# Expert lists scattered into DRAM slots, and gate logits and ranks in a PSUM bank of their own

## The chip, the cores and the metric

The kernel runs on one core of a Trainium2 chip. The metric is device time in microseconds (us). The kernel before took 1025.91 us, the median of 3 executions (1025.23 to 1027.11). Engines are named as the profile names them: PE (matrix multiply), PEld (its weight load), DVE (vector), ACT (scalar), POOL, SP (which issues most DMAs).

## The reference

Local attention in chunks of 64 tokens over 8 heads of 64, for 8 x 576 = 4608 tokens, gives x of 512 values per token. A mixture of 8 experts follows, of which each token uses two:

```
logits = x @ w_gate
noise_scale = np.log1p(np.exp(x @ w_noise))
noisy_logits = logits + noise_scale * noise
top2 = np.argpartition(-noisy_logits, 2, axis=1)[:, :2]
top2_w = softmax over the two                      # (shortened)
for e in range(E):
    for k in range(2):
        mask = top2[:, k] == e
        h = np.maximum(x[mask] @ w1[e], 0.0)       # 512 -> 1024
        out[mask] += top2_w[mask, k, None] * (h @ w2[e])   # 1024 -> 512
```

All of it is in 32-bit floats. To know which rows an expert gets, the kernel needs for each expert a list: which token stands in its slot 0, 1, 2 and so on, with which weight.

## The kernel before

**Attention.** Tokens go in 36 tiles of 128. `attend(it)` is a software pipeline: in one call it issues scores (L407), max, subtract and exp (L411, L416, L419) of tile `it`, the transpose of an older tile, the product with v (L434) and the normalisation on DVE (L439, L442, L446) of older ones still, then the transpose (L454) and the store of x to the DRAM buffer `xbuf`. Every fourth call issues the gate matmul (L461, L472). PSUM has 8 banks: scores in 0 and 1, the product with v in 3 and 4, the gate matmul in 6. The gate's logits and the ranks stand in the free columns of bank 3 or 4, by turns with the group. PE, DVE and ACT guard PSUM against each other by whole banks.

**Routing.** Tokens are routed in five groups of 8, 8, 4, 8, 8 tiles. `route(g)` is a generator: each `next` issues a small piece, so that it lies between attention's instructions (`step_route`, 10 steps in an attend). It finds the two experts (MAX, MAX_INDEX), counts by two kinds of matmuls how many earlier tokens chose each expert (rank), and writes `lii` (L572), the slot number of each token and choice: rank times 8 plus the expert. `vals` holds the pair to be listed, token number and weight.

**Lists.** A list is built by one-hot matmuls. Per token tile POOL (L595) and ACT (L596, L597) make one-hot matrices of the slot's row, DVE (L599) one-hots of its column and expert, POOL (L603; DVE for the last group) multiplies these with `vals`, and PE adds 128x160 products in PSUM bank 7 (`place`, L587). The profile has 4 rows of L587 for a tile, 144 in all. At a group's end DVE adds the bank into `acc` (L619, L621). `EARLY` starts expert 0 before all groups are known: block 0 after group 1, block 1 after group 3, block 2 after group 4. `finish_lists` (L202 to L206, DVE) turns list entries into row numbers and weights; `gather` (L235, POOL) fetches the rows by indirect DMA. After the last group four DVE pairs (L634, L636) sort the lists by expert size, and `finish_lists` runs for all lists; `pieces` then computes the row numbers for later gathers (L255).

**Experts.** Each expert has 1152 to 1216 slots in blocks of about 384. `layer1` makes 8 slices (f) of h, each 4 x 3 matmuls (three products of high and low parts in reduced precision, L300), then ACT writes hh (L318) and DVE hl (L319), its low part. `layer2` makes a tile of 128 rows from 8 slices; DVE weighs it (L338), POOL stores it by an indirect DMA that adds (L267). Layer 1 of block 0 issues the last attends from a hook, with a step of routing in the other hooks; layer 2 of block 0 and layer 1 of block 1 step the routing too. `finish_route` issues what is left before layer 2 of block 1.

**Order.** The schedule is manual: each engine runs its instructions in the order in which the code issues them and waits for semaphores. An instruction that waits holds up all behind it on its engine. SP's DMAs stand in one queue: loads of q, k and v, weights of expert 0, zeroing of the output (L665, 37 of 256 KB), then the later weights.

Of the kernel before, what the change touches and what calls it, by code (L numbers as in the profile page):

```python
# [8 lines left out]
FT = mybir.dt.float32  # L9
# [10 lines left out]
P = 128  # L20
# [3 lines left out]
NE = 8  # L24
# [36 lines left out]
def kernel(ctx, tc, qT, kT, vh, wgn, noise, w1, w2, out, caps=CAPS):  # L61
# [18 lines left out]
    row = consts.tile([P, P], FT, name="row")  # L80
    nc.gpsimd.iota(row, pattern=[[1, P]], base=0, channel_multiplier=0, allow_small_or_imprecise_dtypes=True)
    e_row = row[:, 0:NE]

    row_p = consts.tile([P, P], FT, name="row_p")
    nc.gpsimd.iota(row_p, pattern=[[NE, P]], base=0, channel_multiplier=0, allow_small_or_imprecise_dtypes=True)
    row_je = consts.tile([P, NLIST, NE], FT, name="row_je")
    nc.gpsimd.iota(row_je, pattern=[[NE * P, NLIST], [1, NE]], base=0, channel_multiplier=0, allow_small_or_imprecise_dtypes=True)
# [76 lines left out]
    NL = NJ * NE  # L164
    acc = consts.tile([P, 2, NL], FT, name="acc")
# [12 lines left out]
    opieces = out.rearrange("r (q c) -> (r q) c", c=P)  # L178
    HF = {}
# [210 lines left out]
    nc.sync.dma_start(xbuf[0:P, :], zero)  # L390
    load_q(3)
# [26 lines left out]
    def soft_exp(t):  # L418
        nc.scalar.activation(PR[t], PR[t], AF.Exp, scale=0.125)  # L419
# [45 lines left out]
    def lg_at(t):  # L465
        g = grp_of[t]
        c = 264 + 16 * (t - groups[g][0])
        return PS[:, 3 + g % 2, c:c + 16]
# [7 lines left out]
    def route(g):  # L476
# [8 lines left out]
        lg = PS[:, 3 + g % 2, 264:264 + 16 * G].rearrange("p (g a e) -> p g a e", a=2, e=NE)  # L485
# [45 lines left out]
        rk = PS[:, 3 + g % 2, 400:400 + 8 * (G + 1)].rearrange("p (g e) -> p g e", e=NE)  # L531
# [43 lines left out]
        pj = gate.tile([P, 2, 2, G], I32, name="gpj")  # L575
        pf = gate.tile([P, 2, 2, G], FT, name="gpf")
        V.tensor_scalar(pj[:, 0], lii[:, :, ts], NE * (P - 1), None, op0=OP.bitwise_and)
        V.tensor_tensor(pj[:, 1], lii[:, :, ts], pj[:, 0], OP.subtract)
        V.tensor_copy(pf, pj)  # L579
        yield  # L580

        lp = PS[:, 7, 0:2 * NL]
        built = []

        def place(r, ohp, rhs):
            for k in range(2):
                nc.tensor.matmul(lp, ohp[:, k], rhs[:, k].rearrange("p c n -> p (c n)"),  # L587
                                 start=(r == 0 and k == 0), stop=(r == G - 1 and k == 1))

        B = nc.gpsimd if g < LAST else V  # L590
        n2 = [P, 2, NL]
        for r in range(G):
            t = t0 + r
            ohp = gate.tile([P, 2, P], FT, name="gohp", bufs=3)
            nc.gpsimd.tensor_scalar(ohp[:, 0], row_p, pf[:, 0, 0, r:r + 1], None, op0=OP.is_equal)  # L595
            nc.scalar.activation(ohp[:, 1], row_p, AF.Abs, scale=-1.0, bias=pf[:, 0, 1, r:r + 1])  # L596
            nc.scalar.activation(ohp[:, 1], ohp[:, 1], AF.Relu, scale=-1.0, bias=1.0)  # L597
            eq = gate.tile(n2, FT, name="geq", bufs=3)
            V.tensor_tensor(eq, row_je.rearrange("p j e -> p (j e)")[:, None, :].to_broadcast(n2),  # L599
                            pf[:, 1, :, r:r + 1].to_broadcast(n2), OP.is_equal)  # L600
            yield
            rhs = gate.tile([P, 2, 2, NL], FT, name="grhs", bufs=3)
            B.tensor_tensor(rhs, eq[:, :, None, :].to_broadcast([P, 2, 2, NL]),  # L603
                            vals[:, :, t, :, None].to_broadcast([P, 2, 2, NL]), OP.mult)
            yield
            yield
            built.append((r, ohp, rhs))
            if len(built) > 2:
                yield
                place(*built.pop(0))  # L610
            yield
        while built:
            for _ in range(3):
                yield
            place(*built.pop(0))
        yield
        av = acc.rearrange("p c n -> p (c n)")
        if g == 0:
            V.tensor_copy(av, lp)  # L619
        else:  # L620
            V.tensor_add(av, av, lp)  # L621
        a4 = acc.rearrange("p c (j e) -> p c j e", e=NE)
        for i in EARLY:
            if g == EARLY[i]:
                js = slice(blocks[0][i][0][0], blocks[0][i][-1][0] + 1)
                finish_lists(lid0[i], lwt0[i], lfl[:, js, 0], a4[:, :, js, 0])
                gather(i)
        if g == LAST:
            for c in range(2):
                for js in (slice(0, NJ // 2), slice(NJ // 2, NJ)):  # L630
                    n = [P, js.stop - js.start, NE, NE]
                    by = gate.tile([P, 2, 2, NL], FT, name="grhs", bufs=3).rearrange("p a b n -> p (a b n)")
                    by = by[:, 0:n[1] * NE * NE].rearrange("p (j r e) -> p j r e", r=NE, e=NE)
                    V.tensor_tensor(by, a4[:, c, js][:, :, None, :].to_broadcast(n),  # L634
                                    perm[:, None].to_broadcast(n), OP.mult)
                    V.tensor_reduce(accp[:, c, js], by, AX.X, OP.add)  # L636
                    yield
            finish_lists(lid, lwt, lfl, accp)
# [14 lines left out]
    def finish_route(until=lambda: not routing):  # L653
        while not until():
            step_route(1)

# [10 lines left out]
    def attend(it):  # L667
# [58 lines left out]
    def hook_tail(f, d):  # L726
        if d == 0 and f % 2 == 0 and f >= 2:
            if f == 2:
                zero_out(10)
            zero_out(9)  # L730
        if d % 2 and tail and (f, d) != (0, 3):
            attend(tail.pop(0))
        else:
            step_route(2)

    for i in range(NBL + 1):
# [40 lines left out]
        if i < NBL:  # L777
            layer1(i, hook1, hook_tail if i == 0 else lambda f, d: step_route(1))
# [160 lines left out]
```

## Time and profile before

| | |
|---|---|
| Median of 3 (lowest to highest) | 1025.91 us (1025.23 to 1027.11) |
| Profiled execution | 1026.64 us |
| its span | 1024.7 us |
| its mean granted PE clock | 0.977 |
| PE busy | 970.7 us (95%) |
| DVE, ACT, POOL busy | 461.7, 300.8, 475.5 us |

The profile is one execution. Its page gives busy times and groups of instructions by line; L12 is line 12 of the kernel before. "Idle before" is the time in which the engine stood before instructions of this group, with what ended it. A timeline row is start, duration, engine, line, operation, tiles, and in brackets the idle time just before and its releaser.

### The profile page before, as it was taken

Reading aid. Unit: us, or ns where it says so; the run is one execution under the profiler, and the core shown is the slowest. Engines: PE = TensorE matmul, PEld = TensorE weight load, DVE = VectorE, ACT = ScalarE, POOL = GpSimd, SP = SyncE. Lnnn points to the kernel's source line nnn. Section 1 sums busy time; section 2 is a strip of 40 time slices with the busy share of each in tenths; the row PEclk is TensorE's granted clock in tenths of the full one; section 3 lists DMA queues with packets and bytes.
Section 4 is the critical chain, followed back from the end, with each engine's and each line's share of the span. In section 5 each row is a group of like instructions: output and inputs, shape, how many; then the busy total and the mean of one; then the engine's idle time right before and its main releaser. Section 6 shows DMA issues by size and latency. Waiting matters only on the chain.

```text
span 1024.7 us, 18328 instructions
## 1 busy us (share of the span) xinstructions
PE 970.7 (95%) x7353; PEld 864.3 (84%) x7353; DVE 461.7 (45%) x1037; ACT 300.8 (29%) x649; POOL 475.5 (46%) x613
## 2 busy tenths in 40 slices
PE   6888978999799999999999999999999999999995
PEld 4677757898679899889988998899989998899884
DVE  5587765644334444344424533453245334434311
ACT  3466644331223232123212321231123222323100
POOL 1043523425767467436743775378336734611111
PEclk9889989999899999999999999999999999999998
DMA  9997891232251335233533353335333434412213
GB/s 365 397 326 275 302 380 43 46 95 75 60 141 44 88 89 137 49 82 90 135 49 83 98 128 55 83 101 126 55 104 97 98 66 105 124 27 31 32 21 42
DMA packets 51943, 121.51 MB, mean 119 GB/s; under 512 B 8288, under 2 KB 9184, under 8 KB 51856
## 3 DMA queue, kind: packets, MB, share of 16 engines
q0 software_dynamic: 20160, 38.69, 20.6%
q1 hardware_dynamic: 26512, 72.20, 19.3%
q10 hardware_dynamic: 5184, 9.44, 2.4%
q8 instruction: 58, 0.95, 0.4%
q14 instruction: 29, 0.24, 0.1%
HBM read 81.56 MB, written 38.73 MB: 117 GB/s over the span
## 4 chain that ended last, share of the span: by engine, by line
PE 87%; DVE 5%; DMA 3%; issue 2%; ACT 1%; SPq 1%; POOL 0%; DVEq 0%; ACTq 0%
PE PS L300 79%; DMA out<-zero 2%; PE PS L587 1%; PE PS L434 1%; PE PS L407 1%; SPq L665 1%; PE PS L423 1%; PE PS L329 1%; DVE xs L446 1%; DVE pr L416 1%; DVE mx L411 1%; PE PS L454 1%; PE PS L472 1%; DMA st<-in_w 1%; PE PS L461 0%
## 5 line engine op out<-in xcount | busy, mean ns | idle before, releaser
L255 POOL DMA_INDIRECT xg<-xbuf,piece x257 | 259.4, 1009 | 77.2 <-issue 62.3
L300 PE MATMUL PS<-xh,w1h 128*128 128x384 f32 (+2 forms) x768 | 264.0, 344 | 4.3 <-issue 1.9
L300 PE MATMUL PS<-xh,w1l 128*128 128x384 f32 (+2 forms) x768 | 261.9, 341 | 2.5 <-issue 2.5
L300 PE MATMUL PS<-xl,w1h 128*128 128x384 f32 (+2 forms) x768 | 262.1, 341 | 1.6 <-issue 1.3
L300 PE MATMUL PS<-w2h,hh 128*128 128x512 f32 x584 | 228.7, 392 | 0.0
L300 PE MATMUL PS<-w2h,hl 128*128 128x512 f32 x584 | 227.8, 390 | 0.1
L300 PE MATMUL PS<-w2l,hh 128*128 128x512 f32 x584 | 227.7, 390 | 0.0
L267 POOL DMA_INDIRECT out<-o,lid x73 | 116.8, 1600 | 227.8 <-DVE o L338 208.8
L319 DVE SCALAR_TENSOR_TENSOR hl<-PS,hh 128x384 fp32r<-128x384 f32 (+1 forms) x192 | 107.1, 559 | 246.1 <-ACT hh L318 185.2
L318 ACT ACTIVATE hh<-PS 128x384 fp32r<-128x384 f32 (+1 forms) x192 | 94.0, 491 | 374.7 <-PE PS L300 316.7
L300 PEld LDWEIGHTS PS<-xh,w1h 128*128 128x128 f32 x768 | 145.2, 189 | 9.0 <-issue 3.8
L300 PEld LDWEIGHTS PS<-xl,w1h 128*128 128x128 f32 x768 | 145.1, 189 | 5.4 <-issue 3.0
L300 PEld LDWEIGHTS PS<-xh,w1l 128*128 128x128 f32 x768 | 145.2, 189 | 3.4 <-issue 2.4
L338 DVE TENSOR_SCALAR o<-PS,lwt 128x512 f32<-128x512 f32 x73 | 54.5, 749 | 190.3 <-PE PS L300 153.5
L300 PEld LDWEIGHTS PS<-w2h,hl 128*128 128x128 f32 x584 | 109.2, 187 | 23.9 <-issue 0.5
L300 PEld LDWEIGHTS PS<-w2h,hh 128*128 128x128 f32 x584 | 109.2, 187 | 23.1 <-issue 0.8
L300 PEld LDWEIGHTS PS<-w2l,hh 128*128 128x128 f32 x584 | 109.2, 187 | 22.8 <-issue 0.4
L290 ACT ACTIVATE xh<-y 128x512 fp32r<-128x512 f32 x67 | 41.2, 614 | 101.2 <-DVE y L287 72.8
L291 DVE TENSOR_TENSOR xl<-y,xh 128x512 fp32r<-128x512 f32 x67 | 44.9, 671 | 48.0 <-ACT xh L290 33.5
L595 POOL TENSOR_SCALAR gohp<-row_p,gpf 128x128 f32<-128x128 f32 x36 | 24.2, 674 | 71.8 <-DVE gpf L579 54.2
L287 DVE STREAM_TRANSPOSE y<-xg 128x512 f32<-128x512 f32 x67 | 45.6, 680 | 0.0
L136 DVE TENSOR_TENSOR w2l<-st,w2h 128x512 fp32r<-128x512 f32 x64 | 44.5, 695 | 0.0
(138 smaller groups left out, 788.6 us busy)
## 6 DMA issues: line engine op xcount, KB each, us to landing
st<-in_w SPq DMA_DIRECT2D x64, 512.0 KB
out<-zero SPq DMA_DIRECT2D x37, 256.0 KB
vb<-in_vh SPq DMA_DIRECT2D x18, 520.0 KB
qp<-in_qT SPq DMA_DIRECT2D x18, 512.0 KB
kb<-in_kT SPq DMA_DIRECT2D x18, 512.0 KB
xbuf<-xs ACTq DMA_DIRECT2D x36, 256.0 KB
xg<-xbuf,piece POOLq DMA_INDIRECT x257
out<-o,lid POOLq DMA_INDIRECT x73
```

The costliest lines, as they stand in the source:

```text
L136: (eng or nc.vector).tensor_sub(lo[:, s], st[:, s], hi[:, s].bitcast(FT))
L255: nc.gpsimd.indirect_dma_start(out=XG[e, j][:, t * P:(t + 1) * P], out_offset=None, in_=xpieces, in_offset=bass.IndirectOffsetOnAxis(ap=pi ...
L267: s = nc.gpsimd.indirect_dma_start(out=to, out_offset=bass.IndirectOffsetOnAxis(ap=rows, axis=0), in_=o, in_offset=None, compute_op=OP.add)
L287: nc.vector.transpose(y[:, 0:4 * r], x[:, 0:4 * r])
L290: nc.scalar.activation(oh, src, AF.Copy)
L291: nc.vector.tensor_sub(ol, src, oh.bitcast(FT))
L300: nc.tensor.matmul(p, a, b, start=first and n == 0, stop=last and n == 2)
L318: nc.scalar.activation(hh[:, 0:m], p, AF.Relu)
L319: nc.vector.scalar_tensor_tensor(hl[:, 0:m], p, 0.0, hh[:, 0:m].bitcast(FT), op0=OP.max, op1=OP.subtract)
L329: nc.tensor.matmul(p[32 * q:32 * q + 32, 0:P], HF[0][:, f, 32 * t:32 * t + 32], w[:, q * P:(q + 1) * P], start=(f == 0), stop=(f == NF - 1))
L338: nc.vector.tensor_scalar(o[0:r], p[0:r], weights_of(i, j)[0:r], None, op0=OP.mult)
L595: nc.gpsimd.tensor_scalar(ohp[:, 0], row_p, pf[:, 0, 0, r:r + 1], None, op0=OP.is_equal)
```

## The change

The list matmuls and everything that feeds them (L574 to L621) are removed. After `lii` is written, 16 (group 2: 8) entries go into a FIFO of closures, `moves`. Each is `place_one(t, k)`: a POOL memset of one element and an indirect DMA that writes 128 rows of 8 bytes, (token, weight), from `vals` to the DRAM tensor `lists` at the slots `lii[:, k, t]`: 72 scatters. They are declared independent of each other. A DMA of SP at the start zeroes the slots (82 KB). After the scatters of groups 1 and 3 follow an SP DMA that reads expert 0's part into `acc0[i]`, five empty moves, and finish_lists with gather; after those of group 4 an SP DMA of all lists into `acc` (128 x 10 runs of 64 bytes), five empty moves, finish_lists and gather for block 2, the four reorder pairs as moves, and the full finish_lists. Moves are taken 3 at a time in an attend, one in each hook of layer 1 of block 0, and one in every second hook of layer 2 of block 0 and layer 1 of block 1. Logits and ranks are moved into bank 7, which has no other use until `pieces`.

```
-        lg... PS[:, 3 + g % 2, 264 + ...]          rk = PS[:, 3 + g % 2, 400:...]
+        c = 128 * (g % 2) + 16 * (t - groups[g][0])
+        return PS[:, 7, c:c + 16]
+        rk = PS[:, 7, 256:256 + 8 * (G + 1)]...
...
+    nc.sync.dma_start(slots.rearrange("(p a) c -> p (a c)", p=P), zero[:, 0:2 * NJ * NE])
...
-        for r in range(G):
-            ... gohp (L595 to L597), geq (L599), grhs (L603), place (L587)
-        V.tensor_copy(av, lp) / V.tensor_add(av, av, lp)
+        moves.extend(lambda t=t, k=k: place_one(t, k) for t in range(t0, t0 + G) for k in range(2))
         for i in EARLY:
-            if g == EARLY[i]:
-                finish_lists(...); gather(i)
+            if g == EARLY[i] and g < LAST:
+                moves.append(lambda i=i, js=js: read.append(nc.sync.dma_start(acc0[i], by_slot[:, js, 0, :])))
+                moves.extend([None] * 5)
+                moves.append(lambda i=i, js=js: (finish_lists(lid0[i], lwt0[i], lfl[:, js, 0], acc0[i]...), gather(i)))
         if g == LAST:
+            moves.append(lambda: nc.sync.dma_start(acc.rearrange("p j e c -> p j (e c)"),
+                                                   by_slot.rearrange("p j e c -> p j (e c)")))
+            moves.extend([None] * 5)
+            ... finish_lists and gather(2), four reorder moves, finish_lists(lid, lwt, lfl, accp)

+    def place_one(t, k):
+        nc.gpsimd.memset(spacer, 0.0)
+        d = nc.gpsimd.indirect_dma_start(
+            out=lists, out_offset=bass.IndirectOffsetOnAxis(ap=lii[:, k, t:t + 1], axis=0),
+            in_=vals[:, k, t, :].bitcast(I32), in_offset=None)
...
+        step_moves(3 if it <= NT else 0)         # attend, after soft_exp
+        step_moves(1)                            # hook_tail (layer 1 of block 0)
+            step_moves(1 - f % 2)                # hook2_r (layer 2 of blocks 0 and 1)
+  lambda f, d: (step_route(1), step_moves(1 - d % 2))   # layer 1 of block 1
```

The order of instructions moves at three places (lines of the changed kernel are shifted by one to three: L200 to L204 there are finish_lists, L410, L415 and L438 to L445 the attention's DVE work, L317 is hl, L336 the weighing). First DVE in attention, where the list of block 0 is finished. Before, behind the normalisation in the attend of tile 31 and ahead of that tile's max; `acc` is the sum of the list matmuls:

```order
L446 TENSOR_TENSOR xs<-PS,rc 128x2x4x64
L621 TENSOR_TENSOR acc<-acc,PS 128x160
L202 COPY lwt_121<-acc 128x3
L203 TENSOR_SCALAR lfl<-acc,col 128x3
L204 SCALAR_TENSOR_TENSOR lfl<-acc,lfl 128x3
L205 TENSOR_SCALAR lfl<-lfl,col 128x3
L206 CAST lid_118<-lfl 128x3
L411 TENSOR_REDUCE mx<-PS 128x8
L416 TENSOR_TENSOR pr<-PS,mx 128x2x4x64
```

The changed kernel, after tile 33's subtraction; `acc_111` is `acc0[0]`, which SP's read fills, and the copy waits for that DMA:

```order
L410 TENSOR_REDUCE mx<-PS 128x8
L415 TENSOR_TENSOR pr<-PS,mx 128x2x4x64
L200 COPY lwt_119<-acc_111 128x3
L201 TENSOR_SCALAR lfl<-acc_111,col 128x3
L202 SCALAR_TENSOR_TENSOR lfl<-acc_111,lfl 128x3
L203 TENSOR_SCALAR lfl<-lfl,col 128x3
L204 CAST lid_116<-lfl 128x3
L438 TENSOR_SCALAR rc<-PS 128x8
```

The list of block 0 moves nearly three attends later in the order, and what follows on DVE is the normalisation (L438) in the attend of tile 34. Group 1's `lii` moves one attend earlier.

Second, DVE in layer 1 of block 1, where the list of block 2 is finished. Before, behind hl of the last slice:

```order
L319 SCALAR_TENSOR_TENSOR hl_3142<-PS,hh_3141 128x384
L621 TENSOR_TENSOR acc<-acc,PS 128x160
L202 COPY lwt_123<-acc 128x4
L203 TENSOR_SCALAR lfl<-acc,col 128x4
L204 SCALAR_TENSOR_TENSOR lfl<-acc,lfl 128x4
L205 TENSOR_SCALAR lfl<-lfl,col 128x4
L206 CAST lid_120<-lfl 128x4
```

The changed kernel, from hl of slice 4 (`hl_2992`) to hl of slice 6 (`hl_2996`):

```order
L317 SCALAR_TENSOR_TENSOR hl_2992<-PS,hh_2991 128x384
L200 COPY lwt_121<-acc 128x4
L201 TENSOR_SCALAR lfl<-acc,col 128x4
L202 SCALAR_TENSOR_TENSOR lfl<-acc,lfl 128x4
L203 TENSOR_SCALAR lfl<-lfl,col 128x4
L204 CAST lid_118<-lfl 128x4
L317 SCALAR_TENSOR_TENSOR hl_2994<-PS,hh_2993 128x384
L589 TENSOR_TENSOR gby<-acc,gperm 128x320
L591 TENSOR_REDUCE gaccp<-gby 128x40
```

The copy from `acc` now stands ahead of hl of slices 5 to 7, with the reorder pairs between these. The list of block 1 likewise stands between hl of slices 4 and 5 of layer 1 of block 0 (before between slices 6 and 7).

Third, POOL where the gather of block 2 stands (`lid_118` is its list in the changed kernel). It follows the last scatters, five of which stand behind the third store of block 0:

```order
L607 MEMSET spacer 1x1
L608 DMA lists<-vals,lii 44032x2
L233 DMA xg<-xbuf,lid_118 128x512 x3
L233 DMA xg<-xbuf,lid_118 64x512
L264 MEMSET spacer 1x1
L265 DMA out<-o,lid_117 4736x512
```

Before, the last one-hots of POOL stood there:

```order
L595 TENSOR_SCALAR gohp<-row_p,gpf 128x128 x5
L235 DMA xg<-xbuf,lid_120 128x512 x3
L235 DMA xg<-xbuf,lid_120 64x512
L266 MEMSET spacer 1x1
L267 DMA out<-o,lid_119 4736x512
```

So on POOL scatters take the places of one-hots, ahead of the same gathers and stores. On SP the read for block 0 stands between the first and second w2 load of expert 0, that for block 1 behind 28 of the 37 zeroing DMAs, and that of all lists behind the w1 loads of expert 1.

More of the change, by code (lines that the diff above doesn't have):

```diff
@@ L79 @@
     spacer = consts.tile([1, 1], FT, name="spacer")
-    row = consts.tile([P, P], FT, name="row")
-    nc.gpsimd.iota(row, pattern=[[1, P]], base=0, channel_multiplier=0, allow_small_or_imprecise_dtypes=True)
+    row = consts.tile([P, NE], FT, name="row")
+    nc.gpsimd.iota(row, pattern=[[1, NE]], base=0, channel_multiplier=0, allow_small_or_imprecise_dtypes=True)
     e_row = row[:, 0:NE]
[L84 to L87, printed above, removed]
     vals = consts.tile([P, 2, NT, 2], FT, name="vals")
@@ L161 @@
     xg = ctx.enter_context(tc.tile_pool(name="xg", bufs=5))
-    NL = NJ * NE
-    acc = consts.tile([P, 2, NL], FT, name="acc")
+    acc = consts.tile([P, NJ, NE, 2], FT, name="acc")
+    acc0 = {b: consts.tile([P, len(blocks[0][b]), 2], FT, name=f"acc0{b}") for b in EARLY if EARLY[b] < 4}
     lid = consts.tile([P, NJ, NE], I32, name="lid")
@@ L178 @@
     opieces = out.rearrange("r (q c) -> (r q) c", c=P)
+    slots = lists[0:NJ * P * NE, :].bitcast(FT)
+    by_slot = slots.rearrange("(j p e) c -> p j e c", p=P, e=NE)
+    placed, read = [], []
     HF = {}
@@ L466, in lg_at @@
         g = grp_of[t]
-        c = 264 + 16 * (t - groups[g][0])
-        return PS[:, 3 + g % 2, c:c + 16]
+        c = 128 * (g % 2) + 16 * (t - groups[g][0])
+        return PS[:, 7, c:c + 16]
     def gate_sum(g):
@@ L530, in route @@
             yield
-        rk = PS[:, 3 + g % 2, 400:400 + 8 * (G + 1)].rearrange("p (g e) -> p g e", e=NE)
+        rk = PS[:, 7, 256:256 + 8 * (G + 1)].rearrange("p (g e) -> p g e", e=NE)
         nc.tensor.matmul(rk, before, ohb, start=True, stop=False)
@@ L574, in route @@
         yield
[L575 to L579, printed above, removed]
-        yield
[L582 to L588, printed above, removed]
@@ L590, in route @@
-        B = nc.gpsimd if g < LAST else V
-        n2 = [P, 2, NL]
-        for r in range(G):
[L593 to L623, printed above, removed]
-            if g == EARLY[i]:
-                js = slice(blocks[0][i][0][0], blocks[0][i][-1][0] + 1)
-                finish_lists(lid0[i], lwt0[i], lfl[:, js, 0], a4[:, :, js, 0])
-                gather(i)
@@ L628, in route @@
[L628 to L638, printed above, removed]
+        moves.extend(lambda t=t, k=k: place_one(t, k) for t in range(t0, t0 + G) for k in range(2))
@@ new lines, in route, with reorder @@
+        for i in EARLY:
+            if g == EARLY[i] and g < LAST:
+                js = slice(blocks[0][i][0][0], blocks[0][i][-1][0] + 1)
+                moves.append(lambda i=i, js=js: read.append(nc.sync.dma_start(acc0[i], by_slot[:, js, 0, :])))
+                moves.extend([None] * 5)
+                moves.append(lambda i=i, js=js: (finish_lists(lid0[i], lwt0[i], lfl[:, js, 0], acc0[i].rearrange("p j c -> p c j")),
+                                                 gather(i)))
+        if g == LAST:
+            a4 = acc.rearrange("p j e c -> p c j e")
+            def reorder(c, js):
+                n = [P, js.stop - js.start, NE, NE]
+                by = gate.tile([P, NJ * NE * NE // 2], FT, name="gby", bufs=2)
+                by = by[:, 0:n[1] * NE * NE].rearrange("p (j r e) -> p j r e", r=NE, e=NE)
+                V.tensor_tensor(by, a4[:, c, js][:, :, None, :].to_broadcast(n),
+                                perm[:, None].to_broadcast(n), OP.mult)
+                V.tensor_reduce(accp[:, c, js], by, AX.X, OP.add)
+            moves.append(lambda: nc.sync.dma_start(acc.rearrange("p j e c -> p j (e c)"),
+                                                   by_slot.rearrange("p j e c -> p j (e c)")))
+            moves.extend([None] * 5)
+            for i in EARLY:
+                if EARLY[i] == LAST:
+                    js = slice(blocks[0][i][0][0], blocks[0][i][-1][0] + 1)
+                    moves.append(lambda i=i, js=js: (finish_lists(lid0[i], lwt0[i], lfl[:, js, 0], a4[:, :, js, 0]), gather(i)))
+            moves.extend(lambda c=c, js=js: reorder(c, js) for c in range(2) for js in (slice(0, NJ // 2), slice(NJ // 2, NJ)))
+            moves.append(lambda: finish_lists(lid, lwt, lfl, accp))
@@ new lines, in route @@
+        yield
+    moves = []
+    def place_one(t, k):
[3 more added lines that the diff above has]
+            in_=vals[:, k, t, :].bitcast(I32), in_offset=None)
+        for o in placed:
+            tc.declare_no_dep(d.ins, o.ins, reason="each token and expert has a slot of its own")
+        for o in read:
+            tc.declare_no_dep(d.ins, o.ins, reason="slots that were read are not written afterwards")
+        placed.append(d)
@@ L640, with step_moves @@
+    def step_moves(n):
+        for _ in range(n):
+            if moves:
+                move = moves.pop(0)
+                if move:
+                    move()
     routing = []
@@ L651, with finish_route @@
     ordered = []
-    def finish_route(until=lambda: not routing):
+    def finish_route(until=lambda: not routing and not moves):
         while not until():
             step_route(1)
+            step_moves(1)
     halves = [(c, h) for c in range(4) for h in range(2)]
@@ L734, in hook_tail @@
             step_route(2)
+        step_moves(1)
     for i in range(NBL + 1):
@@ L777 @@
         if i < NBL:
-            layer1(i, hook1, hook_tail if i == 0 else lambda f, d: step_route(1))
+            layer1(i, hook1, hook_tail if i == 0 else lambda f, d: (step_route(1), step_moves(1 - d % 2)))
         split1 = halves if (i < NBL and b == nb - 1 and e + 1 < NE) else []
```

2 lines of the change are left out of this document (1 added, 1 removed).

## The prediction

> **What bounds the kernel now.** I read the busy line first, then a table of stretches, the groups, the chain of waits in the attention stage, and the timelines of PE, POOL and DVE. The table's columns are the stretch in us, its length, and each engine's busy time and instructions, then the granted clock, the DMA share and GB/s.
>
> ```profile
> PE 970.7 (95%) x7353; PEld 864.3 (84%) x7353; DVE 461.7 (45%) x1037; ACT 300.8 (29%) x649; POOL 475.5 (46%) x613
> ...
> 38.00:70.00 32.00, 27.23 (x658) 22.68 (x657) 23.77 (x82) 18.93 (x39) 7.64 (x6) 0.87 0.99 371
> 75.00:100.00 25.00, 22.43 (x526) 18.29 (x516) 19.29 (x71) 16.10 (x39) 9.38 (x13) 1.00 0.81 275
> 100.00:125.00 25.00, 23.59 (x493) 20.15 (x491) 17.53 (x53) 15.91 (x40) 10.71 (x16) 0.93 0.84 291
> 125.00:150.00 25.00, 19.44 (x367) 14.80 (x365) 17.30 (x67) 12.57 (x31) 8.45 (x11) 0.86 1.04 392
> 187.00:208.00 21.00, 19.76 (x102) 15.87 (x101) 14.52 (x73) 4.82 (x12) 8.50 (x11) 1.00 0.32 63
> 208.00:247.00 39.00, 37.85 (x216) 34.77 (x214) 17.94 (x45) 9.19 (x21) 13.47 (x15) 1.00 0.35 95
> 247.00:275.00 28.00, 22.20 (x88) 17.65 (x87) 6.74 (x11) 4.14 (x8) 19.70 (x26) 0.82 0.28 58
> 275.00:1024.70 749.70, 737.45 (x3969) 667.98 (x3967) 298.41 (x494) 182.00 (x380) 380.04 (x484) 0.99 0.35 82
> ```
>
> From 275 us on PE is busy 98% of the time, with work that the change doesn't touch. So the answer is decided before: attention until 149 us, then expert 0's first blocks to 250. There PE is at 78 to 94% in attention and 94 to 97% between 187 and 247. List work is on PE's chain in the stage where the lists are built, 73.1 to 112 us:
>
> ```profile
> by line: PE PS L587 13.2%; PE PS L423 10.3%; PE PS L434 9.8%; PE PS L407 9.7%; PE PS L454 7.2%; DVE xs L446 5.3%; DVE mx L411 4.7%; issue 4.5%; PE PS L472 4.2%; DVE pr L416 3.2%; DVE gmi L515 2.9%; ACT xt L455 2.8%; PE PS L461 2.6%; ACT pts
> ```
>
> **What is removed.** The groups give the list work that goes (busy us, mean ns):
>
> ```profile
> L587 PE MATMUL PS<-grhs,gohp 128*128 128x160 f32 x144 | 25.1, 306 | 0.8 <-POOL grhs L603 0.8
> L595 POOL TENSOR_SCALAR gohp<-row_p,gpf 128x128 f32<-128x128 f32 x36 | 24.2, 674 | 71.8 <-DVE gpf L579 54.2 <-PE PS L587 16.4 <-ACT xt L455 1.2
> L603 POOL TENSOR_TENSOR grhs<-geq,vals 128x320 f32<-128x320 f32 x28 | 20.4, 728 | 2.6 <-DVE geq L599 2.2 <-DVE rc L439 0.3
> L596 ACT ACTIVATE gohp<-row_p,gpf 128x128 f32<-128x128 f32 x36 | 14.2, 396 | 22.2 <-DVE gpf L579 12.1 <-PE PS L587 10.0
> L599 DVE TENSOR_TENSOR geq<-row_je,gpf 128x160 f32<-128x160 f32 x36 | 12.1, 345 | 0.2
> L439 DVE TENSOR_SCALAR rc<-PS 128x8 f32<-128x8 f32 x36 | 5.7, 159 | 16.7 <-PE PS L472 13.9 <-PE PS L434 2.7
> ```
>
> The 306 ns is not the price on PE, since starts overlap. PE's timeline (start, us) shows it, together with the pace of attention, whose tiles start with L407 (tiles 10, 18, 19 and 35), and the first work of expert 0's blocks (L283).
>
> ```profile
> 39.55 1.13 PE L407 MATMUL PS<-kb,qp 64*64 64x64 f32 x32
> 68.26 0.69 PE L407 MATMUL PS<-kb,qp 64*64 64x64 f32 x32
> 73.14 0.86 PE L407 MATMUL PS<-kb,qp 64*64 64x64 f32 x32
> 76.95 1.35 PE L587 MATMUL PS<-grhs,gohp 128*128 128x160 f32 x8
> 142.12 0.69 PE L407 MATMUL PS<-kb,qp 64*64 64x64 f32 x32 [1.06 <-DVE pr L416]
> 149.09 1.09 PE L283 MATMUL PS<-ident,xg 128*128 128x128 f32 x8
> ...
> 172.06 0.70 PE L587 MATMUL PS<-grhs,gohp 128*128 128x160 f32 x4
> 172.49 0.45 PE L300 MATMUL PS<-xh,w1h 128*128 128x384 f32 x1
> 172.78 0.34 PE L300 MATMUL PS<-xl,w1h 128*128 128x384 f32 x1
> 172.95 0.34 PE L300 MATMUL PS<-xh,w1l 128*128 128x384 f32 x1
> ```
>
> Attention: groups 0 to 2 hold 20 token tiles, 4 rows each, 80 rows by 1.35/8 = 0.17 us: 13.5 us of PE. By pace: tiles 10 to 18 take (68.26 - 39.55)/8 = 3.59 us each without list matmuls, tiles 19 to 35 take (142.12 - 73.14)/16 = 4.31; 0.72 by 16 = 11.5. I take **12**. In the layers a tile's 4 rows push the next matmul back by 0.43 (172.06 to 172.49) and stretch it by 0.29 - 0.17 = 0.12; 16 tiles (groups 3 and 4) by 0.55 = **9**. The list work of POOL, ACT and DVE lies beside this in the pace, and is not counted again.
>
> Logits and ranks in bank 7: rc waited 13.9 us for L472, a gate matmul that shares its bank. Between 0 (PE was 90% busy around it) and 13.9; PE itself seldom waited there, so I take **1**. The new bank is shared by logits and ranks of adjacent groups, both off the attention chain: 0.
>
> Other edits at nothing: the zeroing of 82 KB at the start lies under loads; the smaller iotas run ahead of the first tile. The DMA engines look full (1.04), but 37 zeroing transfers of 256 KB, 9.7 MB, are in it and are due only before the first store. Without them, 75 to 150 us moved 25 x (275 + 291 + 392) = 23.9 less 9.7 MB, 14.2 MB; in 62 us that is 229 GB/s against the 371 seen. The cover gone, that is rival two.
>
> **What is added.** 72 scatters of 128 rows of 8 bytes, each with a memset, in POOL's order. Before has no plain scatter; the nearest rows are gathers (not accumulating) and stores (scattering with add):
>
> ```profile
> 244.83 0.95 POOL L255 DMA_INDIRECT xg<-xbuf,piece  x1 [0.30 <-issue]
> 261.07 1.62 POOL L267 DMA_INDIRECT out<-o,lid  x1 [0.22 <-issue]
> 262.11 0.62 POOL L266 MEMSET spacer<- 1x1 f32 x1
> 263.00 1.58 POOL L267 DMA_INDIRECT out<-o,lid  x1 [0.27 <-issue]
> ```
>
> So the period p of scatters lies between 0.95 + 0.30 = 1.25 us and 263.00 - 261.07 = 1.93. Store and scatter share the direction, gather and scatter the lack of an add; I take **p = 1.3**, gather-like because both copy 128 rows without an add, and keep 1.93.
>
> The lists then hang on a chain of POOL, DMA, SP and DVE: lii written (L572), 16 scatters, their landing, SP's read, and finish_lists, a fixed place in DVE's order. Behind the waiting copy (L202 before) stand attention's max, subtract and normalise, or hl (L319), for which PE waits. When lii came for groups 1, 3 and 4, when layer 1 reached hh of slice 4 (block 0) and hl of slice 7 (block 1), and how late a store's packets go:
>
> ```profile
> 103.55 0.29 DVE L572 TENSOR_REDUCE lii<-gohr 128x16 int32<-128x128 f32 x1
> 163.76 0.28 DVE L572 TENSOR_REDUCE lii<-gohr 128x16 int32<-128x128 f32 x1
> ...
> 178.65 0.47 ACT L318 ACTIVATE hh<-PS 128x384 fp32r<-128x384 f32 x1
> ...
> 202.97 0.26 DVE L572 TENSOR_REDUCE lii<-gohr 128x16 int32<-128x128 f32 x1
> ...
> 228.43 0.56 DVE L319 SCALAR_TENSOR_TENSOR hl<-PS,hh 128x384 fp32r<-128x384 f32 x1 [2.08 <-ACT hh L318]
> ...
> 195.25 1.64 POOL L267 DMA_INDIRECT out<-o,lid  x1 [3.57 <-DVE gex L526]
> ...
> GB/s 197 262 131 16 16 0 16 16 0 0 0 0 0 0 0 0 0 57 82 82 106 139 180 205 148 41 8 0 0 0 0 0 0 0 0 0 0 0 0 0
> ```
>
> (the last row cuts 193 to 203 us into 40: the store issued at 195.25 moves data from 197.3 to 199.8, 4.5 us after issue). 8-byte rows carry 1 KB where that store carried 256 KB; estimates between 2 and 4.5, I take 3 to land and 2.5 for the read.
>
> The Trainium skill, "DMA: Bandwidth & Descriptors", section "Anatomy of one DMA — SWDGE (gpsimd) path", puts the fixed cost of such a transfer at about 2.0 us, mostly the write receipt. By that the total would be about 1 us lower; the store's 4.5 us doesn't contradict it, as it includes 256 KB.
>
> *Group 1* feeds block 0. In the new pace tile 25 starts at about 73 + 6 x 3.59 = 94.5; its lii now stands there, at 95. POOL has done group 0 by 70 + 16p = 91. Sixteen by 1.3 are 21 us (three moves per tile allow 19): 116, plus 5.5 = 121.5. DVE asks after 23 moves, behind tile 33: 73 + 14 x 3.59 + 1 = 124. Stall 0.
> *Group 3* feeds block 1. Attention ends 13 us earlier (136 for the L283 at 149.09), and its lii, now ahead of hl of slice 0, moves to about 141. 141 + 20.8 + 5.5 = 167.3. DVE asks behind hl of slice 4: 178.65 - 13, less the list matmuls of five slices, 163. Two slices of about 3 us fit in PSUM meanwhile: stall 1.
> *Group 4* feeds block 2 and all later lists. In block 1, hl of slice 7 would stand at 228.43 - 22 + 1 = 207.5, layer 1 having 12 matmuls by 0.173, 2.1 us, a slice; its start is 17 us before, at 191. The last 5 scatters stand behind the third store of block 0, which follows that start by some 3 us: 194 + 6.5 + 3 = 203.5; the read of 1280 runs of 64 bytes, an estimate, takes 3 to 6 us: 206.5 to 209.5. DVE asks behind hl of slice 4, near 201; hl of slices 5 to 7 wait, with finish_lists and four reorder pairs between, 7.6 us of DVE work. Layer 2 of block 1, from 208, needs the last of them 5 us in, at 213. Stall 1 to 4 by this, 7 if the stores ahead run late: **5.5**, toward the upper end, since each delay ahead of it adds to it.
>
> **Sum.** 12 + 9 + 1 - 0 - 1 - 5.5 = 15.5. The profiled execution took 1026.64 (span 1024.7 plus 1.9), 0.7 over the median shown: 1026.6 - 15.5 = 1011.1, to be compared with medians as **1011**.
>
> **Rivals.**
> 1. *The scatter costs like the store, p = 1.93.* For: it is the only write in the trace. Against: that one adds. Group 0 ends at 70 + 31 = 101, group 1 at 101 + 31 + 5.5 = 137.5 against 124: 13.5; group 3 stalls 1 + 16 x 0.63 = 11, group 4 5.5 + 5 x 0.63 = 8.7: 33 in all. 1026.6 - 22 + 33 - 0.7 = **1037**, slower. It decides from p of about 1.72, where the stalls reach 22.
> 2. *The list matmuls were covered.* DVE (19.29 of 25) or the transfers set attention's pace. For: the transfers' 0.99 in the stretch that I took as free of lists (38 to 70). Against: tiles 19 to 35 slow by just what L587 takes. Attention then gains 3 rather than 13: **1021**.
> 3. *A stall that isn't in the change's reach goes or grows.* Between 247 and 275 PE lost 5.8 us at clock 0.82 in an unchanged order. If it vanishes with the new timing, **1003**; the same amount could come anew.
> 4. *DVE holds up descriptor writing.* Were each scatter held for half a DVE instruction (0.345/2 by L599), p would be near 1.5, the stalls 0 + 4.2 + 6.5: **1015**. The gather at 126.7 us does not show it with DVE 69% busy:
>
> ```profile
> 126.68 0.95 POOL L235 DMA_INDIRECT xg<-xbuf,lid  x1 [0.30 <-issue]
> ```
>
> That rule is the Trainium skill's, "SBUF — State Buffer", section "SBUF: two separate sides": descriptors from POOL can't be written while DVE runs an operation that takes both ports. The row disagrees so far.
>
> **How the numbers follow.** Forecast 0.56, rival one 0.23, two 0.12, three 0.05, four 0.04. The likeliest one's own range is 1004 to 1019 (read 3 to 6, bank 0 to 4, pace 9 to 14, p 1.25 to 1.5). To leave out 2 in 10, I reach to 1002 below and to 1033 above, part way into rival one, whose stalls shrink if scatters cost between gather and store. 0.2%, 2 us, is about what a measurement here can tell from none. Slower: rival one less its cheaper part, 0.19, and 0.04 of new stalls: 0.23. Same: 0.07. Faster: 0.70.
>
> **What would show it.** Right: no L587, tiles 19 to 35 at about 3.6 us, scatters 1.3 apart, no wait of DVE at the first finish_lists, a wait of some us at the third, and 275 us onward unchanged. The bank's term is right if rc has no wait for the gate sum. Wrong: a long wait of DVE at its copies from acc0 with scatters 1.9 apart (rival one); a pace above 4 us with full transfers (two).

## The result, and the profile after

The changed kernel takes **1079.01 us**, the median of 4 runs (1077.33 to 1082.25), against 1025.57 for the kernel before, the median of 4 beside them (1024.66 to 1027.11). The ratio is **1.0523**, with a 95% interval of 1.0493 to 1.0554: slower by 5.2%. Forecast was 1011, with a range of 1002 to 1033.

The profiled execution has a span of 1080.5 us. Its page, busy time by engine and the granted clock of PE in 40 slices of 27 us:

```profile
span 1080.5 us, 17954 instructions
PE 978.5 (91%) x7209; PEld 863.2 (80%) x7209; DVE 444.7 (41%) x973; ACT 278.7 (26%) x577; POOL 509.9 (47%) x691
PEclk9976785688999999999999999999999999999997
```

PE, DVE and ACT execute fewer instructions than before, yet PE is busy longer, at a clock that is low between 54 and 270 us and in the last slice. The table of stretches shows the same; columns as in the prediction (PE, PEld, DVE, ACT, POOL, granted clock, DMA share, GB/s):

```profile
75.00:100.00 25.00, 16.89 (x165) 11.41 (x163) 6.43 (x14) 6.67 (x12) 15.61 (x28) 0.57 0.34 115
100.00:125.00 25.00, 18.71 (x438) 15.16 (x437) 16.33 (x70) 10.97 (x27) 7.33 (x14) 0.84 0.72 246
125.00:150.00 25.00, 14.08 (x256) 10.71 (x256) 10.11 (x43) 5.83 (x11) 9.39 (x18) 0.65 0.30 91
...
200.00:225.00 25.00, 10.77 (x68) 9.10 (x69) 3.71 (x9) 2.98 (x6) 11.37 (x21) 0.59 0.27 92
...
325.00:1080.00 755.00, 740.60 (x3981) 671.18 (x3979) 301.55 (x500) 183.37 (x384) 385.68 (x489) 0.99 0.36 82
```

From 75 to 100 us PE executed 165 matmuls; the kernel before executed 526 in the same stretch. DVE, ACT and the transfers idle with it. From 325 us on the two kernels run alike. So the time went into the part where the lists are made, while no engine but POOL had more to do there.

What PE waited for, in the list of waits of the changed kernel (total us, times, longest):

```profile
PE PS L433 <- issue: 22.6, 33, 2.4
PE PS L406 <- issue: 9.4, 14, 1.7
PE PS L422 <- issue: 6.4, 7, 2.4
```

and the longest such rows of the kernel before:

```profile
PE PS L300 <- issue: 5.7, 6, 1.6
PE PS L434 <- issue: 4.1, 5, 2.1
PE PS L407 <- issue: 1.5, 1, 1.5
```

"issue" is a wait for nothing that the profile shows: no semaphore, engine or transfer is seen to be late, and yet the next matmul doesn't start. All rows of this kind together are 52 us on PE, 11 before. POOL's and PE's timelines beside each other show when. POOL first, the scatters of group 1 from the first to the last:

```profile
116.36 0.97 POOL L608 DMA_INDIRECT lists<-vals,lii  x1 [19.50 <-DVE vals L572]
117.33 0.09 POOL L607 MEMSET spacer<- 1x1 f32 x1
117.63 0.97 POOL L608 DMA_INDIRECT lists<-vals,lii  x1 [0.22 <-issue]
...
135.43 0.96 POOL L608 DMA_INDIRECT lists<-vals,lii  x1 [0.22 <-issue]
```

PE in the same time (one row is a run of matmuls; x4 means four of the 32 that one tile has on this line):

```profile
115.62 0.65 PE L433 MATMUL PS<-vb,pts 64*64 64x65 f32 x32
...
122.11 0.45 PE L433 MATMUL PS<-vb,pts 64*64 64x65 f32 x4 [1.09 <-issue]
123.55 0.47 PE L433 MATMUL PS<-vb,pts 64*64 64x65 f32 x3 [0.99 <-issue]
124.99 0.49 PE L433 MATMUL PS<-vb,pts 64*64 64x65 f32 x4 [0.98 <-issue]
...
139.67 1.06 PE L453 MATMUL PS<-ident,xs 128*128 128x128 f32 x4
140.66 1.13 PE L406 MATMUL PS<-kb,qp 64*64 64x64 f32 x32
```

At 115.62, 32 matmuls took 0.65 us. Two us into the run of scatters PE falls to three or four matmuls per 1.44 us, later to fewer, and some 4 us after the last scatter was issued it is back at full pace. The scatters themselves come 1.27 us apart (117.63 - 116.36), as forecast.

The kernel before has one place that looks much the same, and the prediction had looked at it without knowing its cause. POOL issues 14 gathers and 2 stores back to back from 243.5 us, and some 17 us later (not 2, as in attention) PE does this:

```profile
260.20 0.37 PE L300 MATMUL PS<-xh,w1h 128*128 128x448 f32 x1
260.63 0.47 PE L300 MATMUL PS<-xl,w1h 128*128 128x448 f32 x1
262.05 0.36 PE L300 MATMUL PS<-xh,w1l 128*128 128x448 f32 x1 [0.95 <-issue]
263.46 0.36 PE L300 MATMUL PS<-xh,w1h 128*128 128x448 f32 x1 [1.05 <-issue]
264.89 0.53 PE L300 MATMUL PS<-xl,w1h 128*128 128x448 f32 x1 [1.08 <-issue]
```

It goes on at 269, when POOL has stopped:

```profile
267.59 0.96 POOL L255 DMA_INDIRECT xg<-xbuf,piece  x1 [0.30 <-issue]
271.32 0.18 POOL L248 COPY spacer<-hh 1x1 f32<-1x1 f32 x1 [2.78 <-ACT hh L318]
```

### The profile page after: what moved, and what is told of

The parts are those of the page before. It is cut to its first block, busy times and chain, and to the rows that moved or that the text cites. A ratio compares the mean times of both kernels' runs of the same rounds, so it can differ in the third digit from the quotient of the medians.

```text
span 1080.5 us, 17954 instructions
## 1 busy us (share of the span) xinstructions
PE 978.5 (91%) x7209; PEld 863.2 (80%) x7209; DVE 444.7 (41%) x973; ACT 278.7 (26%) x577; POOL 509.9 (47%) x691
## 3 DMA queue, kind: packets, MB, share of 16 engines
q1 hardware_dynamic: 28752, 72.37, 18.6%
## 4 chain that ended last, share of the span: by engine, by line
PE 83%; DVE 6%; another core or an unknown queue 5%; issue 4%; ACT 1%; DMA 0%; SPq 0%; DVEq 0%; ACTq 0%
PE PS L298 74%; PE PS L433 2%; PE PS L406 2%; PE PS L422 1%; DVE mx L410 1%; DVE pr L415 1%; PE PS L453 1%; PE PS L327 1%; DVE xs L445 1%; PE PS L460 1%; PE PS L471 1%; PE PS L281 0%; DVE gmi L514 0%; DMA kb<-in_kT 0%
## 5 line engine op out<-in xcount | busy, mean ns | idle before, releaser
L317 DVE SCALAR_TENSOR_TENSOR hl<-PS,hh 128x384 fp32r<-128x384 f32 (+1 forms) x192 | 106.8, 558 | 259.2 <-ACT hh L316 182.7
L298 PEld LDWEIGHTS PS<-xh,w1h 128*128 128x128 f32 x768 | 146.2, 190 | 13.5 <-ACT xh L288 6.5
L336 DVE TENSOR_SCALAR o<-PS,lwt 128x512 f32<-128x512 f32 x73 | 54.5, 749 | 193.4 <-PE PS L298 160.0
L608 POOL DMA_INDIRECT lists<-vals,lii x72 | 70.0, 972 | 57.0 <-DVE vals L572 40.6
L433 PE MATMUL PS<-vb,pts 64*64 64x65 f32 x1152 | 39.8, 249 | 32.8 <-issue 22.6
L433 PEld LDWEIGHTS PS<-vb,pts 64*64 64x64 f32 x1152 | 31.1, 157 | 40.4 <-issue 26.9
```

The source lines that it names most:

```text
L298: nc.tensor.matmul(p, a, b, start=first and n == 0, stop=last and n == 2)
L317: nc.vector.scalar_tensor_tensor(hl[:, 0:m], p, 0.0, hh[:, 0:m].bitcast(FT), op0=OP.max, op1=OP.subtract)
L336: nc.vector.tensor_scalar(o[0:r], p[0:r], weights_of(i, j)[0:r], None, op0=OP.mult)
L433: nc.tensor.matmul(PS[s, 3 + h, hp * 65:hp * 65 + 65], PT[t][r, hp, s], v[r, t % 2, c, hp, :], start=True, stop=True)
L608: d = nc.gpsimd.indirect_dma_start(out=lists, out_offset=bass.IndirectOffsetOnAxis(ap=lii[:, k, t:t + 1], axis=0), in_=vals[:, k, t, :].bi ...
```

## Experiments

The theories were these. **A**: while POOL issues indirect DMAs without a pause, PE isn't given its instructions. **B**: writes of 8 bytes to DRAM clog the DMA engines. **C**: DVE and POOL wait for the lists, as the prediction's sums of stalls had it. **D**: the shared PSUM bank costs the time. The kernel before ran beside each of them on the same chip; each time is one run where no interval stands. Kernels 1 to 4 ran on one chip, 5 to 8 on another, 9 to 12 on a third, so differences between these groups are the less certain ones.

To take the scatters away without taking the lists away, several kernels fill the DRAM slots once at the start with made-up lists (slot s of every expert holds token s with weight 0.5), so what follows the lists has as much work on other rows:

```
+    made = consts.tile([P, NJ, NE, 2], FT, name="made")
+    nc.gpsimd.iota(made, pattern=[[1, NJ], [0, NE], [0, 2]], base=P - MID, channel_multiplier=NJ, ...)
+    nc.gpsimd.memset(made[:, :, :, 1:2], 0.5)
-    nc.sync.dma_start(slots.rearrange("(p a) c -> p (a c)", p=P), zero[:, 0:2 * NJ * NE])
+    nc.sync.dma_start(slots.rearrange("(p a) c -> p (a c)", p=P), made.rearrange("p j e c -> p (j e c)"))
```

**1. No scatters.** `place_one` does nothing; made-up lists.

> The changed kernel without its 72 scatters and their memsets; the slots are filled once at the start with made-up lists (slot s of each expert holds token s, weight 0.5), so everything behind the lists runs as before. Theory A (a run of indirect DMAs that POOL issues back to back keeps PE from getting its instructions): the time falls to about 1004 us, 1026 less the 22 us that the list matmuls and the bank cost by the prediction, and PE's waits put down to issue fall from 52 us to about 10. Theory B (the 8-byte writes to DRAM clog the DMA engines): the same. Theory C (DVE and POOL wait for the lists): the same, since the lists are there early. Theory D (logits and ranks in one bank cost the time): it stays above 1060.

Measured: 1003.62, with 1021.54 for the kernel before, so 17.9 faster. What the prediction had as gains is there; the 72 scatters cost all of it and 53 us more. D falls.

**2. Scatters that nobody reads.** As 1, with the scatters back in their places, into another tensor:

```
+    spare = dram.tile([LROWS * NE, 2], I32, name="spare")
-            out=lists, out_offset=bass.IndirectOffsetOnAxis(ap=lii[:, k, t:t + 1], axis=0),
+            out=spare, out_offset=bass.IndirectOffsetOnAxis(ap=lii[:, k, t:t + 1], axis=0),
```

> As the kernel without scatters, but the 72 scatters are back in their places with the same rows, into a DRAM tensor that nobody reads; the lists come from the made-up slots. Nobody waits for a scatter. Theory A and theory B: about 1075, within 10 us of the changed kernel's 1079, with PE's issue waits near 50 us. Theory C: about 1005, as without scatters.

Measured: 1069.81, 66 us above kernel 1, though nothing waits for a scatter. PE's issue waits are 49 us (16 without scatters). The longest row in kernel 1, without scatters:

```profile
PE PS L436 <- issue: 8.7, 10, 2.1
```

and of the same matmuls here:

```profile
PE PS L437 <- issue: 19.9, 37, 2.4
```

C falls as the main cause.

**3. Gathers in place of scatters.** As 2, but 128 rows of 8 bytes are read from the slots into SBUF.

```
-            out=spare, out_offset=bass.IndirectOffsetOnAxis(ap=lii[:, k, t:t + 1], axis=0), in_=vals[...]
+            out=fetched[:, k, t, :], out_offset=None, in_=lists[0:NJ * P * NE, :],
+            in_offset=bass.IndirectOffsetOnAxis(ap=lii[:, k, t:t + 1], axis=0))
```

> As the one before, but each scatter is a gather: 128 rows of 8 bytes from the slots into SBUF, by the same indices, from the same place in POOL's order, read by nobody. Theory A: again about 1075 with issue waits near 50 us, since POOL issues as densely. Theory B: about 1005 to 1015, since nothing is written to DRAM.

Measured: 1072.81. Reading costs what writing costs, and B falls.

**4. The old banks.** The changed kernel with logits and ranks in banks 3 and 4 again.

> The changed kernel with logits and ranks back in banks 3 and 4. Theories A to C: 1079 plus 0 to 5 us. Theory D: 1040 or less.

Measured: 1080.75. Beside the changed kernel's 1079.01 (another comparison) no difference can be told. The waits show that the bank did what it is for; in these kernels, where PE is held up anyway, nothing measurable hung on it. In this kernel, with the old banks:

```profile
DVE rc L438 <- PE PS L471: 11.6, 6, 4.5
```

In the changed kernel no row of rc names L471.

**5. A busy POOL without DMAs.** In the place of each scatter POOL runs a memset and two multiplications, 1.3 us.

```
-        d = nc.gpsimd.indirect_dma_start(...)
+        nc.gpsimd.tensor_tensor(pad[:, 1], pad[:, 0], pad[:, 0], OP.mult)
+        nc.gpsimd.tensor_tensor(pad[:, 1, 0:160], pad[:, 0, 0:160], pad[:, 0, 0:160], OP.mult)
```

> The kernel with made-up lists and no scatters; in the place of each scatter and memset POOL runs a memset and two multiplications on a scratch tile, about 1.3 us in all, so POOL is as busy and issues no DMA. If it is the issuing of DMAs that holds PE up: 1004 to 1008, PE's issue waits near 16 us. If a busy POOL is enough: about 1070.

Measured: 1009.78, 15.9 below the kernel before (1025.70) and 1.8 above the 1004 to 1008 expected; PE's issue waits are 13 us. It is the DMAs, not POOL's being busy.

**6. Sixteen rows instead of 128.** As 2, with `lii[0:16, ...]` and `vals[0:16, ...]`.

> The kernel with 72 scatters that nobody reads (1070), each of 16 rows in place of 128. If the cost goes with the rows (descriptors): scatters come 0.4 to 0.6 us apart, and the time is 1004 to 1020. If it goes with the number of DMAs: 1050 to 1070.

Measured: 1071.47, as with 128 rows. The forecast of 0.4 to 0.6 us between scatters was wrong: they hardly get shorter with an eighth of the rows, as POOL's timeline shows.

```profile
88.56 0.85 POOL L612 DMA_INDIRECT spare<-vals,lii  x1 [0.22 <-issue]
...
89.71 0.84 POOL L612 DMA_INDIRECT spare<-vals,lii  x1 [0.22 <-issue]
```

So the price goes with the DMAs and how densely they stand, not with rows or bytes.

**7. Scatters 1.8 us apart.** As 2, with one multiplication on a scratch tile behind each:

```
         placed.append(d)
+        nc.gpsimd.tensor_tensor(pad[:, 1, 0:200], pad[:, 0, 0:200], pad[:, 0, 0:200], OP.mult)
```

> The kernel with 72 scatters that nobody reads (1070), with a multiplication on a scratch tile behind each, so that they come about 1.8 us apart instead of 1.27. If PE is held up only in an unbroken run and a pause of half a microsecond lets it go on: 1005 to 1020. If each scatter costs PE its own share (66 us by 72, 0.9 us each): about 1070 again.

Measured: 1026.48, between the two forecasts, against about 1070 without the pause: more POOL work, and 44 us less. On the same chip the dense 16-row kernel took 1071.47 and kernel 5 1009.78; of these 62 us the pause of half a microsecond takes away 45.

**8. The same mean rate in groups of four.** Three multiplications behind every fourth scatter, none behind the others.

> As the one before, at the same mean rate, but four scatters 1.27 apart and then a pause of about 2 us. If a run must be some 5 us long before PE is held up: 1005 to 1015, less than with even spacing. If each scatter costs its share: about 1070.

Measured: 1048.17, again between the forecasts. Four in a row already hold PE up; the even pause is better by 22 us.

**9 and 10. Half of the scatters, dense and spaced.** Only the 36 of the first choice; once dense, once with two multiplications behind each (2.75 us apart).

> The kernel with made-up lists and scatters that nobody reads, with only the 36 scatters of the first choice (8 in a group, 1.27 us apart). If PE is held up in proportion to the length of dense runs: 1004 plus half of 66, about 1035. If a run of 10 us is too short to hold it up: 1004 to 1012.

> The same 36 scatters, with two multiplications on a scratch tile behind each (1.5 us), so that they are about 2.75 us apart and POOL is busy as long as with 72 dense ones. If the pause between DMAs decides: 1004 to 1010, less than the dense half. If each scatter has its price: the same as the dense half.

Measured: 1028.81 dense, 1012.72 spaced, beside 1026.25 (median of 13 of the kernel before). The dense half misses both of its forecasts: against kernels 1 and 10 its 36 scatters cost 16 to 20 us, under a third of the 66 that 72 cost, so a longer dense run costs more per scatter. The same 36 scatters differ by 16 us with the pause between them. Against the kernel before the spaced half stands at -13.5 us, next to -17.9 for kernel 1 and -15.9 for kernel 5, so little is left of their price, though 1012.72 lies above the 1004 to 1010 expected.

**11. The changed kernel, spaced.** The multiplication of 7 behind each scatter of the changed kernel, with real lists.

> The changed kernel with its real lists, and the same 0.55 us multiplication behind each scatter that brought the unread scatters from 1070 to 1026. If the pause works here too, the lists still come later than the prediction had them with p = 1.3: by its own sums 3 to 15 us of waiting in DVE on top of 1026, 1029 to 1041, with a wait of DVE at the copy for block 0. If the time of the changed kernel is mostly such waiting: above 1070.

Measured: 1045.85, above the 1029 to 1041 expected and far below 1079. Here C has its share: where PE's long stalls are gone, DVE waits for the lists. The list of DVE's waits:

```profile
DVE lwt L202 <- DMA acc<-lists: 18.6, 2, 10.6
```

Kernel 7, whose lists are made up, has 6.8 us of this wait, all at block 2, so the scattered lists account for 11.8 of the 19.4 us between the two kernels, which ran on different chips. The two waits are at blocks 1 and 2; that at block 0, which was expected, did not come.

**12. The gathers of the kernel before, spaced.** If A holds, the stall near 260 us of the kernel before must go when its 14 gathers are spaced:

```
-                gathered(3, 3)
+                while quarters and quarters[0][0:2] <= (3, 3):
+                    gather_some(1)
+                    nc.gpsimd.tensor_tensor(jp, row_p, row_p, OP.mult)
+                    nc.gpsimd.tensor_tensor(jp[:, 0:8], row_p[:, 0:8], row_p[:, 0:8], OP.mult)
```

> The kernel before, with the 14 gathers that it issues back to back near 243 us set 1.8 us apart by two small multiplications on a scratch tile behind each. If such a run holds PE up whatever it carries, PE's stall near 260 us (issue waits of 5.7 us, then a slow clock to 275) goes: 1025.6 less 9, plus 0 to 5 for x tiles that now come later, 1016 to 1022. If that stall has another cause: 1025 to 1030.

Measured: 1027.17, ratio 1.0018 (0.9998 to 1.0037): no gain, and yet the stall is gone. In its table of stretches:

```profile
247.00:275.00 28.00, 28.00 (x135) 25.07 (x134) 15.11 (x25) 10.75 (x21) 24.73 (x41) 1.00 0.25 51
...
300.00:350.00 50.00, 44.45 (x314) 38.31 (x313) 22.48 (x38) 15.75 (x36) 30.07 (x42) 0.93 0.25 54
```

PE, 22.20 of 28 us busy there before, has 28.00. The loss came back at 302 to 316 us, where the kernel before has none:

```profile
300.00:350.00 50.00, 50.00 (x366) 45.96 (x365) 23.79 (x40) 16.40 (x38) 30.40 (x41) 1.00 0.25 52
```

POOL was behind with its gathers, issued them densely until it had caught up, and PE stalled again until POOL paused:

```profile
313.74 0.37 PE L300 MATMUL PS<-xl,w1h 128*128 128x448 f32 x1 [1.64 <-issue]
315.87 0.53 PE L300 MATMUL PS<-xl,w1h 128*128 128x448 f32 x1 [0.87 <-issue]
```

and POOL's last gather of the run:

```profile
313.00 0.95 POOL L255 DMA_INDIRECT xg<-xbuf,piece  x1 [0.31 <-issue]
316.68 0.18 POOL L248 COPY spacer<-hh 1x1 f32<-1x1 f32 x1 [2.72 <-ACT hh L318]
```

The pause that frees PE seems to be made by PE's own stall: hh is late, POOL's copy waits for it, and the run ends.

**13. All gathers of six blocks spaced.** The two multiplications behind each quarter gather of the first six blocks behind expert 0.

> The kernel before with the same two small multiplications behind every quarter gather of the first six blocks behind expert 0 (76 gathers), not only behind the first 14, where the stall at 260 us went and one of the same size came at 303 us, when POOL had caught up to dense issue. If the pause between DMAs keeps PE supplied for as long as it is kept: no stall at 260 or at 303, PE busy throughout from 247 to 350, and 1026 less 7 to 9, 1016 to 1020. If a pause only puts the stall off, or x tiles come late from the slower POOL: 1024 to 1030.

Measured: 1026.97, with no issue wait of PE behind 235 us. But the kernel before took 1013.86 beside it (median of 7, 1011.12 to 1020.58), so the ratio is 1.0132 (1.0083 to 1.0181). The slower POOL brought its own wait: stores are late, with them DVE, and PE lost 7.6 us once waiting for hl:

```profile
PE PS L303 <- DVE hl L322: 7.6, 1, 7.6
```

Why the kernel before was about 1% faster in this comparison than in the others was not found; there is no profile of it from there. Its granted clock was 0.982 to 0.994 there, against 0.976 to 0.984 in the next comparison on the same chip, so the stall may have been absent, which is not shown.

**14. A shorter pause.** As 13 with only the first of the two multiplications (1.65 us from gather to gather).

```
+            if i < NPE + 6:
+                nc.gpsimd.tensor_tensor(jp, row_p, row_p, OP.mult)
```

> As the kernel with all gathers of six blocks spaced, but with one multiplication behind each (about 1.65 us from gather to gather in place of 1.85), since there the stalls were gone, and PE lost 7.6 us once near 370 us because stores came late behind the spaced gathers on POOL. If the shorter pause is enough: no issue stall behind 240 us, no late stores, 8 us less than the longer pause. If it is not: issue waits of some us between 250 and 320 again, and no gain.

Measured: **1018.25**, beside 1025.51, ratio **0.9914** (0.9882 to 0.9947): faster than the kernel before beside it. No issue wait is left between 240 and 330 us, and 1.8 us of short ones later; stores are still late, against the expectation (DVE waited 9.6 us once for one). Its stretches:

```profile
247.00:275.00 28.00, 28.00 (x137) 24.82 (x136) 12.70 (x21) 8.75 (x17) 24.95 (x37) 1.00 0.27 54
...
300.00:350.00 50.00, 49.80 (x359) 45.14 (x358) 22.50 (x37) 14.91 (x34) 44.73 (x67) 1.00 0.28 71
```

The gain of 0.9% is smaller than what the kernel before gained by itself in comparison 13, on the same chip (1013.86, less than this kernel's 1018.25), so what shows the mechanism is the trace more than the time.

**15. The kernel before, profiled once more.**

> The kernel before once more, for a profile beside these runs, since it took 1014 on the chip of the last comparison and 1026 on the one before. If the stall near 260 us comes in some executions and not in others: a time below 1020 goes with no issue waits of PE between 250 and 280, one near 1026 with about 6 us of them.

Measured: 1027.65 with 4.7 us of issue waits between 250 and 280, as the second case expected. No execution without the stall was profiled.

## Why the prediction was wrong, point by point

- **The step that failed** is "What is added". It priced a scatter as time on POOL (p) and as a link in a chain of waits, and gave it no price on PE. Kernels 1, 2 and 5 show that price: 66 us for 72 dense scatters that nobody reads, and about 2 us for as much other work on POOL (17.9 against 15.9 below the kernel before). That is 0.92 us a scatter here, but not a fixed price: kernels 7 to 10 show that it depends on the pause and the length of the run. It is more than three times the gain.
- **A row of the profile was set aside.** Rival three called the stall near 260 us one "that isn't in the change's reach", because its instructions don't change. POOL's timeline had the 14 gathers beside it, and kernels 12 and 14 show that these gathers made it: spaced, they leave PE alone between 247 and 275 us. By that it is the same mechanism at work in the kernel before. A mechanism is in a change's reach when the change makes more of its cause.
- **The period of scatters**: taken as 1.3, bounds 1.25 and 1.93, measured 1.27. Right, and gather-like as argued. Rival one, which took the store's 1.93, did not occur, and neither of its signs came: no long wait at the copies, no scatters 1.9 apart. Only its direction, slower, came true, and that by luck.
- **What goes**: 12 + 9 + 1 = 22 forecast. Kernel 1 starts expert 0's blocks 12 us earlier than the kernel before did at 149.09:

```profile
137.12 1.97 PE L281 MATMUL PS<-ident,xg 128*128 128x128 f32 x8
```

  By the first hh of block 1's layer 1 (192.74, before 210.02) it is 17.3 ahead, and by the last 20.6: sizes right. At the end it is 17.9 ahead of a single run of the kernel before. The sum itself was 0.7 us off: 1026.6 - 15.5 is the profiled execution's time, and less the 0.7 that the rivals take off it gives 1010. Rival two (the list matmuls were covered) falls by the same rows.
- **The bank** was given 1 us. Its sign came (rc has no wait for the gate sum), but kernel 4 can't tell its worth from nothing.
- **The list chain**: forecast stalls 0, 1 and 5.5. In the changed kernel DVE waited 1.3 us once,

```profile
DVE lwt L200 <- DMA acc<-lists: 1.3, 1, 1.3
```

  probably because PE's stalls made all who ask for lists late as well. In kernel 1, without a scatter, DVE waited 5.9 us at the third list. That it is near 5.5 is luck: the forecast's wait came from late scatters, this one from the read, which SP begins to issue at 186.07, behind the weight loads, and for which DVE waits until 208.04: 22 us where the prediction took 3 to 6. In kernel 11, where PE is held up less, the waits are 18.6 us where its expectation, by the prediction's sums, had 3 to 15: a step that was low, too.
- **Rival four** (DVE holds up the writing of descriptors) would have made scatters longer; in the changed kernel they take 0.97 us in the median (0.95 to 1.15). Its rule in the Trainium skill, "SBUF — State Buffer", section "SBUF: two separate sides", shows in no run here.
- **The signs named in advance**: tiles at 3.6 us and a wait at the third list would have shown the forecast right. The pace of the tiles failed first, and the alternative named beside it was absent: the DMA share was 0.34, not full, between 75 and 100 us.

## What to carry to other kernels

Indirect DMAs that POOL issues without a pause hold PE up here, after some 2 us in attention and 17 us in the layers, whether they read or write, 16 rows or 128, and whoever waits for them; half a microsecond of other work on POOL between them gives most of it back. Not every run does it: beside ten gathers about 1.3 us apart in the layers of the kernel before, from 803.30 us, PE was busy for all of 803 to 816. Before replacing compute by many small indirect DMAs, count the DMAs in a row, not their bytes, and price them on every engine and not only on the one that issues. And a stall in the profile whose cause is not known should be matched against what the other engines do at that time before it is called outside a change's reach.

## What was not expected of the hardware

- PE, with nothing that the profile shows to wait for, executes 3 or 4 matmuls per 1.44 us beside POOL's dense run in attention, and one per 1.4 us in the layers (262.05, 263.46, 264.89), where otherwise one starts each 0.2 us.
- The pause decides more than the count: 72 scatters cost 66 us at 1.27 us apart (kernel 2 beside kernel 1), 17 us at 1.8 (1026.48 beside 1009.78 for kernel 5, same chip), and 38 us in groups of four at that mean rate (1048.17, beside kernel 5 too).
- An indirect DMA of 16 rows takes 0.85 us of POOL, one of 128 rows 0.97: nearly all of it is fixed.
- Stalls seem to feed on themselves through the clock: with PE held up, its granted clock was 0.57 between 75 and 100 us, where the kernel before had 1.00, so the matmuls that do run are slower, too.
- What exactly is held up is not settled; that PE "isn't given its instructions", as theory A has it, is not shown. Results of PE seem to be late as well: by the timeline the scores of a tile (32 matmuls of L406 from 117.54, 0.69 us) are over at 118.23, and DVE takes their max only at 133.56:

```profile
133.56 0.69 DVE L410 TENSOR_REDUCE mx<-PS 128x8 f32<-128x512 f32 x1 [14.21 <-remote]
```

  "remote" is a releaser that the profile can't name. Such waits of mx and rc are 48.4 us in the changed kernel, 1.0 in the kernel before, 2.8 in kernels 1 and 5 and 6.5 in kernel 7.
- A late fetch of PE's instructions is a suspect. The DMA view of the changed kernel lists for 120 to 139.5 us no packets of the queues of the kind "instruction", which it has before and after. The Trainium skill, "Runtime: NRT & Kernel Launch", section "Instruction fetch mechanics", says that an engine's sequencer fetches the next block of 256 instructions by its own DMA queue while executing the current one, and that this is mostly hidden. The block agrees with the page of the kernel before, if queue 8 is PE's: its 58 packets of 0.95 MB serve 14,706 PE and PEld instructions (2 x 7353), 254 each:

```profile
q8 instruction: 58, 0.95, 0.4%
```

  But the blocks themselves do not look late. In the changed kernel queue 8 has a packet between 116.5 and 117 us and its next one between 140 and 140.5, when PE is already back at full pace (139.67); in the kernel before the first one after the stall comes between 272 and 276, when PE has been going since 269. So PE worked through the stall without a new block and recovered without one. A run that shows what was late was not found.
